# Head-pair keys of batch 0 named ahead of its tail, in a fused linear-attention and feed-forward kernel

## The chip, the cores and the metric

The kernel runs on one core of one Trainium2 chip. The metric is device time in microseconds (us), the median over runs; lower is better. The core has TensorE (PE in the rows; PEld is its weight load), VectorE (DVE), ScalarE (ACT), GpSimd (POOL) and SyncE (SP). SPq and ACTq in the rows are the DMA queues of SyncE and ScalarE.

## The reference

Eight batches of eight heads attend over 576 tokens with 128 random features, and a gated feed-forward layer follows:

```
def phi(x):
    proj = np.einsum('bhsd,df->bhsf', x, w_phi)
    proj = proj - np.max(np.abs(proj), axis=-1, keepdims=True)
    return np.concatenate([np.exp(proj), np.exp(-proj)], axis=-1)
q_p, k_p = (phi(q), phi(k))
kv = np.einsum('bhsf,bhsd->bhfd', k_p, v)
z = np.sum(k_p, axis=2)
num = np.einsum('bhsf,bhfd->bhsd', q_p, kv)
den = np.einsum('bhsf,bhf->bhs', q_p, z)[..., None] + 1e-06
attn = num / den                     # to x: 4608 tokens x 512
h = x @ w_in                         # 512 x 2048
g = h * (1.0 / (1.0 + np.exp(-1.702 * h)))
out = g @ w_out                      # 2048 x 512
```

The inputs are drawn as float32. The weight blocks reach the core 512 KB at a time as 64-bit words, and the kernel turns them into numbers itself.

## The kernel before

**Tiles.** A head pair (hp) is two of the eight heads, so a batch has four pairs. Of a head's 576 tokens 512 are the main part, as 4 groups of 128; the last 64 are the tail. The tails of all heads of a batch are loaded together (`tail_load`, tile `tl`) and made into features in one go (`attn_tail`). Every pair's keys need the tail: the sums over tokens in `keys` take main and tail products into one PSUM bank.

**Precision.** Most operands are split into a high and a low float16 half (`eh` and `el`, `gh` and `gl`, `w16[:, i, 0]` and `[:, i, 1]`), and three products stand for one. For batch 0 the keys of all pairs and the queries of the first half of the tokens (g = 0) go the exact way instead, in float32: `project_whole` turns kt on TensorE against `ident`, multiplies by `wb`, subtracts the maximum (`shifted`), and ScalarE makes the two exponentials. The float16 way (`turned`) writes high and low halves into a tile `xs` and transposes it by DMA into `xT`; the tail and the queries of the second half (g = 1) go that way. Afterwards `across` turns a result of 66 partitions back, and it does so by way of a tile `xs` too.

**Tail queries.** `queries_tail` divides the 64 tail rows of all eight heads. The two heads of a pair lie in the partitions 0 to 63 and 64 to 127. Each half is multiplied, cast and subtracted by itself into a tile `zt`, whose other half has been set to zero once, and `attn_last` brings both to the layout of x with TensorE and the matrix `ii`.

**Weights.** `load_weights(j)` loads block j of w_in and of w_out into `raw`, decodes them on ScalarE and VectorE (through the PSUM tiles `hb` for j below 8) and writes both halves into w16. `moe_chunk` works on up to 384 tokens: products into `hb`, tanh and gate, products into `ab`. The first 512 tokens of batch 0 are done in two parts of eight weight blocks each, so that they can start before all weights are there.

**PSUM.** There are three banks `at` (unordered; `psa()` takes one), two `hb` and three `ab`. In `attention_first` (batch 0), `bank()` takes an `ab`, which the feed-forward layer doesn't need yet.

**Order.** Nothing is issued where it is written. Every operation is recorded in a group, opened by `R.part(v0, v1)`, and `schedule` orders all of them by a planner's costs: it takes, engine by engine, the operation that can start first and, among those that are ready, the one of lowest priority number. The number lies between v0 and v1, by the operation's position in its group and the length of the chain behind it:

```
f = (1 - cp) * i / len(g) + cp * (1 - tail[o] / top)
o.prio = (not o.prio, v0 + (v1 - v0) * f, n)
```

where cp is -0.175 for v0 up to 0.5. For the first 123 groups the pair comes from the table PLACES, by the number of the group, and not from the call. An operation recorded on `two`, `three` or `evac` may go to any of several engines; `price` weighs them. Most tiles have a fixed number of buffers (NB: kt 2, qt 4, vn 2, xs 2, xT 2, raw 3, nf 2, x 3, e 5), which are handed out in the order in which the program names them, unless the name is in `loose` ("sc", "eh", "el", "e", "n1", "cs", "rc", "mq"). All operations carry line 466, where `emit` calls them, so the rows tell them apart by tiles.

**Before the change.** `attention_first` records the weights of the projection (`load_phi`), then the loads of the tail (on ScalarE's queue) and of pair 0, then `attn_tail`, then the four `keys`, the queries of g = 0 and of g = 1, and `queries_tail`.

Of the kernel before, what the change touches and what calls it, by code (L numbers as in the profile page):

```python
# [99 lines left out]
class _Op:  # L100
# [5 lines left out]


PLACES = (
# [25 lines left out]
)  # L134
_READY = {"tensor": 215.0, "scalar": 150.0, "vector": 130.0, "gpsimd": 95.0, "sync": 100.0}

# [38 lines left out]


class Recorder:
    price = dict(tensor=1.000, scalar=0.004, vector=2.234, gpsimd=1.174, sync=1.000)

    def __init__(self, nc):  # L180
        self.nc, self.ops = nc, []
# [291 lines left out]
def attn_moe_fast(ctx, tc, q, k, v, w_phi, w_in, w_out, out):  # L473
# [64 lines left out]
    def new(nm):  # L538
        return R.tile(pools[nm])
# [6 lines left out]
    def new_ex():  # L546

        scr.append(0)
        i = len(scr) % 2
        return scratch[:, 1024 * i : 1024 * i + 1024]  # L550

    def psa():
        return R.tile(at, whole=True)
# [23 lines left out]
    for ap in pools["vts"].aps:  # L577
        nc.vector.memset(ap, 0.0)
        for a in range(2):
            nc.vector.memset(ap[a * D : a * D + D, :, a, 0, D : D + 1], ONE)  # L580
    for ap in pools["zt"].aps:
        nc.vector.memset(ap, 0.0)

    vmx = static("vmx", [P, B], F32)
    wmx = static("wmx", [P, 2 * NJ], F32)
# [221 lines left out]

    def across(src, dst, pat):

        x = new("xs").rearrange("p s i d -> p (s i d)").bitcast(F32)[0:DV]  # L810
        R.evac.copy(x, src)
        tp = psa()[:, 0 : 4 * DV]
        for j in range(4):
            R.tensor.transpose(
                tp[:, j * DV : (j + 1) * DV], x[:, j * P : (j + 1) * P], ident[0:DV, 0:DV]
            )
        R.evac.copy(dst, tp.rearrange(pat, j=2, d=DV))

    def keys(b, hp, kt, vn, tail, nt, exact, keep, bank):
        ekt, eqt, vt, cst = tail  # L820


        if exact:
            tk = project_whole(kt, bank)
            R.three.scale(vn[:, :, 0:D], vn[:, :, 0:D], VS)
            kvt = psa()[0:DV]
            mm = []
            for h in range(2):
                e = new_ex()
                e4 = e.rearrange("p (a s f) -> p a s f", a=4, s=2)  # L830
                R.scalar.activation(e4[:, :, 0], tk[h], AF.Exp)
                R.scalar.activation(e4[:, :, 1], tk[h], AF.Exp, scale=-1.0, bias=-EK * LN2)
                ek = e.rearrange("p (a f) -> p a f", a=4)
                o = kvt[:, 256 * h : 256 * h + 256]
                mm += [(vn[:, 4 * h + t], ek[:, t], o) for t in range(4)]
                for s in range(2):
                    for i, n in ((0, 0), (0, 1), (1, 0)):
                        mm.append((vt[:, hp, h, n], ekt[s][i][:, hp], o[:, s * NF : s * NF + NF]))
            products(mm)
            kf = new("kf")  # L840
            across(kvt, kf, "p (h j d) -> p h j d")
            kf = kf.rearrange("p h s d -> p (h s d)")
# [160 lines left out]
    def queries_tail(nt, cst, x16):  # L1003
# [5 lines left out]
        )  # L1009
        R.vector.reciprocal(rc, rc)  # L1010
        ratio(rc, nt[:, :, D + 1], art[:, 1])
        rcv = rc.rearrange("p (c a) -> p a c", a=2)
        nt4 = nt.rearrange("p (c a) d -> p a c d", a=2)
        xt_ = new("xf").rearrange("p j a d -> p (j a d)")[:, 0 : NHP * D].rearrange(
            "p (c d) -> p c d", c=NHP
        )
        zt = new("zt")
        for a in range(2):
            r = slice(a * D, a * D + D)
            R.two.tensor_mul(  # L1020
                xt_[r], nt4[r, a, :, 0:D], rcv[r, a].unsqueeze(2).broadcast_to([D, NHP, D])
            )
            R.three.copy(zt[r, 0, :, a], xt_[r])
            R.two.tensor_sub(zt[r, 1, :, a], xt_[r], zt[r, 0, :, a])
        attn_last(zt, x16)

    def ratio(rc, z, acc):
# [178 lines left out]
    def attention_first():  # L1206
# [5 lines left out]
        R.part(-20.0, -20.0)  # L1212
        load_phi()
        R.part(-19.9, -19.9)
        tl = tail_load(0, R.scalar)
        nat = [attn_load(0, 0, dv=R.scalar)]
        R.part(-19.8, -19.0)
        nt = new("nt")
        tail = attn_tail(0, tl, bank)
        kk = []  # L1220
        for hp in range(NHP):
            R.part(-19.5 + 0.5 * hp, -19.0 + 0.5 * hp)
            if hp:
                nat.append(attn_load(0, hp))
            kt, qt, vn = nat[hp]
            kk.append(keys(0, hp, kt, vn, tail, nt, EXK[hp], EXQ[0][hp] or EXQ[1][hp], bank))
        for g in range(2):
            for hp in range(NHP):
                w = -17.5 + 0.5 * hp + 8 * g
# [223 lines left out]
```

## Time and profile before

| | us |
|---|---|
| median of three runs | 1065.18 (1064.44 to 1067.8) |
| the profiled execution, its own time | 1066.25 |
| its span, from the first to the last instruction | 1064.5 |
| TensorE busy in the span | 1014.2 |

A row of the timeline gives the start, the duration, the engine, the operation, its output tile and its inputs, how many instructions were merged into it (x8), and in brackets how long the engine had been idle before it and which event ended that. A row of the windows gives a stretch, its length, the busy time of PE, PEld, DVE, ACT and POOL with their instruction counts, the granted TensorE clock as a share of full speed, the DMA share and GB/s. A float32 product is recorded as two instructions.

### The profile page before, as it was taken

To read this page: it belongs to the slowest core of one execution; us is meant where nothing else is said; L and a number is where in the kernel's file an instruction comes from. 1 tells how busy PE (TensorE), PEld (TensorE's weight loads), DVE (VectorE), ACT (ScalarE), POOL (GpSimd) and SP (SyncE) were. 2 spreads that over 40 slices of the span, in tenths; PEclk is the share of its full clock that TensorE was granted. 3 is DMA by queue.
4 is the path that set the end of the run, shared out by engine and by line. 5 is a ranking of instruction groups with operands and counts; after the bars stand their busy time and mean duration, and the time that the engine had idled before them with its cause. 6 is when DMAs were issued, how large, how long until landed. Compare 5 with 4: busy or idle time off the path is not lost.

```text
span 1064.5 us, 24790 instructions
## 1 busy us (share of the span) xinstructions
PE 1014.2 (95%) x9914; PEld 666.7 (63%) x9914; DVE 695.9 (65%) x1278; ACT 663.5 (62%) x1471; POOL 489.2 (46%) x575
## 2 busy tenths in 40 slices
PE   3987999999999999999999999999999999999996
PEld 3655767677665666676666655677766665576543
DVE  5997889887997788888236735656576665223232
ACT  5987989875588698886237735565485554222321
POOL 2218876864387588876006823653463433000000
PEclk6998999999999999999999999999999999999999
DMA  9656264442244264443022321232131120000101
GB/s 262 195 169 176 70 158 110 100 106 61 49 97 94 57 135 94 102 116 76 1 50 62 90 55 31 54 87 51 41 80 23 29 51 11 21 11 1 31 1 33
DMA packets 181021, 80.94 MB, mean 76 GB/s; under 512 B 149536, under 2 KB 174240, under 8 KB 180896
## 3 DMA queue, kind: packets, MB, share of 16 engines
q1 hardware_dynamic: 178048, 78.35, 30.9%
q8 instruction: 79, 1.29, 0.5%
q10 hardware_dynamic: 2848, 0.92, 0.4%
q14 instruction: 46, 0.38, 0.1%
HBM read 45.15 MB, written 9.44 MB: 51 GB/s over the span
## 4 chain that ended last, share of the span: by engine, by line
PE 83%; ACT 6%; DVE 5%; DMA 3%; issue 2%; POOL 1%; ACTq 0%; SPq 0%; DVEq 0%; POOLq 0%
PE ab L466 33%; PE hb L466 32%; PE at L466 17%; DMA xT<-xs 2%; ACT e L466 2%; ACT eh L466 1%; DVE gl L466 1%; DVE sm L466 1%; POOL el L466 1%; ACT x L466 1%; DVE g L466 1%; ACT xs L466 0%; DVE t L466 0%; DMA tl<-in_v_dram 0%; ACT th L466 0%
## 5 line engine op out<-in xcount | busy, mean ns | idle before, releaser
L466 PE MATMUL hb<-x,w 128*128 128x192 f16 (+3 forms) x3264 | 451.7, 279 | 0.7 <-DVE x L466 0.4
L466 PE MATMUL ab<-w,gh 128*128 128x512 f16 x1152 | 337.7, 380 | 0.4 <-ACT gh L466 0.3
L466 PEld LDWEIGHTS <-w 128*128 128x128 f16 x3264 | 276.0, 98 | 95.8 <-issue 1.2
L466 POOL TENSOR_TENSOR el<-e,eh 128x512 f16<-128x512 f32 x168 | 209.1, 1254 | 127.7 <-ACT eh L466 107.0
L466 DVE SCALAR_TENSOR_TENSOR g<-th,hb 128x384 f32<-128x384 f32 (+1 forms) x208 | 107.9, 519 | 179.4 <-ACT th L466 178.6
L466 ACT ACTIVATE th<-hb 128x384 f32<-128x384 f32 (+1 forms) x208 | 96.9, 466 | 193.1 <-PE hb L466 185.1
L466 PE MATMUL ab<-w,gl 128*128 128x512 f16 x576 | 204.3, 379 | 4.2 <-DVE gl L466 4.0
L466 DVE SCALAR_TENSOR_TENSOR gl<-g,gh 128x384 f16<-128x384 f32 (+1 forms) x208 | 136.2, 657 | 50.0 <-ACT gh L466 49.1
L466 PEld LDWEIGHTS <-gh 128*128 128x128 f16 x1152 | 102.4, 98 | 93.9 <-ACT gh L466 16.3
L466 ACT ACTIVATE gh<-g 128x384 f16<-128x384 f32 (+1 forms) x208 | 104.0, 500 | 64.9 <-DVE g L466 64.1
L466 ACT CAST eh<-e 128x512 f16<-128x512 f32 x215 | 128.7, 621 | 3.6 <-PE at L466 3.2
L466 PEld LDWEIGHTS <-eh 128*128 128x128 f16 x1856 | 111.9, 97 | 25.3 <-ACT eh L466 2.7
L466 POOL TENSOR_TENSOR n<-n,cs 128x132 f32<-128x132 f32 (+1 forms) x101 | 58.1, 578 | 98.5 <-ACT n L466 81.1
L466 PEld LDWEIGHTS <-gl 128*128 128x128 f16 x576 | 54.7, 97 | 74.3 <-DVE gl L466 33.2
L466 PEld LDWEIGHTS <-el 128*128 128x128 f16 x928 | 86.2, 98 | 18.7 <-POOL el L466 9.4
L466 PEld LDWEIGHTS <-xT 128*128 128x128 f16 x1056 | 74.6, 99 | 35.9 <-DMA xT<-xs 22.3
L466 PE MATMUL at<-ph,xT 128*128 128x128 f16 x1008 | 94.1, 219 | 0.8 <-DMA xT<-xs 0.6
L466 ACT ACTIVATE e<-t 128x512 f32<-128x512 f32 x128 | 75.9, 625 | 20.2 <-DVE t L466 18.0
L466 ACT ACTIVATE e<-at 128x512 f32<-128x512 f32 x136 | 76.4, 601 | 13.6 <-PE at L466 13.5
L466 PE MATMUL at<-kz,eh 128*128 128x66 f16 x960 | 80.9, 193 | 1.3 <-ACT eh L466 0.7
L466 DVE TENSOR_TENSOR el<-e,eh 128x512 f16<-128x512 f32 x64 | 65.8, 1030 | 24.9 <-ACT eh L466 16.7
L466 PE MATMUL at<-vs,eh 128*128 128x66 f16 x896 | 71.0, 194 | 0.5 <-DVE nf L466 0.5
(179 smaller groups left out, 1349.7 us busy)
## 6 DMA issues: line engine op xcount, KB each, us to landing
raw<-in_moe_w_in_dram SPq DMA_DIRECT2D x16, 512.0 KB, 4.5
raw<-in_moe_w_out_dram SPq DMA_DIRECT2D x16, 512.0 KB, 5.0
kt<-in_k_dram SPq DMA_DIRECT2D x32, 256.0 KB, 2.8
qt<-in_q_dram SPq DMA_DIRECT2D x32, 256.0 KB, 3.1
vn<-in_v_dram SPq DMA_DIRECT2D x62, 128.0 KB, 2.9
out_dram<-e SPq DMA_DIRECT2D x38, 128.0 KB, 2.4
out_dram<-e SPq DMA_DIRECT2D x16, 256.0 KB, 2.6
xT<-xs SPq DMA_TRANSPOSE x68, 2.8
```

The lines of the kernel that those rows point to most:

```text
L466: f(*[g(a) for a in o.args], **{k: g(a) for k, a in o.kw.items()})
```

## The change

Five things change.

1. `keys` is split. The new `keys_front` projects the keys, makes the exponentials and opens the accumulation over the main tokens (eight products, left open); `keys` adds the tail products and closes it. For pairs 0 and 1 of batch 0 the front is named ahead of `attn_tail`, in parts of its own; the load of pair 0 is named ahead of the load of the tail, each in its own part. That makes 126 groups.
2. `attn_tail` of batch 0 takes `at` banks (`psa`) in place of `ab` banks.
3. `across` copies its source into a tile `e` in place of a tile `xs`.
4. `queries_tail` multiplies the reciprocals by a constant `half`, which is 1 for the head that lives in a partition and 0 for the other, and then does one multiplication, one cast and one subtraction over all 512 columns, in place of two of each over 256. The zeros that zt was set to once are now computed, and zt's memset is gone.
5. All places up to the feed-forward layer of batches 2 and 3 are new, and so are three prices.

```diff
-    price = dict(tensor=1.000, scalar=0.004, vector=2.234, gpsimd=1.174, sync=1.000)
+    price = dict(tensor=1.000, scalar=0.001, vector=2.059, gpsimd=1.247, sync=1.000)
...
-    for ap in pools["zt"].aps:
-        nc.vector.memset(ap, 0.0)
+    half = cp.tile([P, 2 * NHP], F32, name="half")
+    nc.vector.memset(half, 0.0)
+    for a in range(2):
+        nc.vector.memset(half[a * D : a * D + D].rearrange("p (c a) -> p c a", a=2)[:, :, a], 1.0)
...
-        x = new("xs").rearrange("p s i d -> p (s i d)").bitcast(F32)[0:DV]
+        x = new("e")[0:DV]
...
+    def keys_front(kt, vn, bank):
+        tk = project_whole(kt, bank)
+        R.three.scale(vn[:, :, 0:D], vn[:, :, 0:D], VS)
+        eks = []
+        for h in range(2):
+            e = new_ex()
+            e4 = e.rearrange("p (a s f) -> p a s f", a=4, s=2)
+            R.scalar.activation(e4[:, :, 0], tk[h], AF.Exp)
+            R.scalar.activation(e4[:, :, 1], tk[h], AF.Exp, scale=-1.0, bias=-EK * LN2)
+            eks.append(e.rearrange("p (a f) -> p a f", a=4))
+        kvt = psa()[0:DV]
+        for h in range(2):
+            o = kvt[:, 256 * h : 256 * h + 256]
+            for t in range(4):
+                R.tensor.matmul(
+                    o, vn[:, 4 * h + t], eks[h][:, t], start=h + t == 0, stop=False,
+                    skip_group_check=True,
+                )
+        return kvt
...
         if exact:
-            tk = project_whole(kt, bank)
-            R.three.scale(vn[:, :, 0:D], vn[:, :, 0:D], VS)
-            kvt = psa()[0:DV]
+            kvt = keys_front(kt, vn, bank) if front is None else front
...
-            products(mm)
+            for i, (st, mv, oi) in enumerate(mm):
+                R.tensor.matmul(
+                    oi, st, mv, start=False, stop=i == len(mm) - 1, skip_group_check=True
+                )
...
+        R.two.tensor_mul(rc, rc, half)
+        xt_ = new("e").rearrange("p (x d) -> p x d", x=2 * NHP)
+        R.two.tensor_mul(
+            xt_, nt[:, :, 0:D], rc.unsqueeze(2).broadcast_to([P, 2 * NHP, D])
+        )
...
+        R.three.copy(zt[:, 0], xt_)
+        R.two.tensor_sub(zt[:, 1], xt_, zt[:, 0])
...
-        tl = tail_load(0, R.scalar)
-        nat = [attn_load(0, 0, dv=R.scalar)]
-        R.part(-19.8, -19.0)
+        nat = [attn_load(0, 0, dv=R.scalar)]
+        R.part(-19.85, -19.85)
+        tl = tail_load(0, R.scalar)
+        NF0 = 2
+        fronts = []
+        for hp in range(NF0):
+            R.part(-19.8 + 0.2 * hp, -19.7 + 0.2 * hp)
+            if hp:
+                nat.append(attn_load(0, hp))
+            fronts.append(keys_front(nat[hp][0], nat[hp][2], bank))
+        R.part(-19.6, -19.0)
         nt = new("nt")
-        tail = attn_tail(0, tl, bank)
+        tail = attn_tail(0, tl, psa)
```

The new places, by group, of those that the prediction speaks of (before, after):

| group | before | after |
|---|---|---|
| load_phi | -91.6 to -64.5 | -319.7 to -277.4 |
| tail load and load of pair 0 | -106.2 to -65.3 (one group) | tail -190.5 to -96.8; pair 0 -292.9 to 143.7 |
| front of pair 0; of pair 1 with its loads | | -328.0 to -90.5; -258.5 to 45.7 |
| attn_tail of batch 0 | -97.6 to -84.4 | -282.9 to -94.9 |
| keys of pairs 0, 1, 2, 3 | -95.6, -94.1, -123.0, -97.6 | -32.8, -29.9, -143.4, -46.2 (starts) |
| queries g = 1 of pairs 0, 1, 2, 3 | -91.0, -97.6, -96.7, -91.7 | -187.2, -111.8, -178.4, -222.1 (starts) |
| weight block 0 | -90.9 to -86.8 | -112.0 to -91.6 |
| weight block 5; 7 | -76.5; -102.2 to -68.2 | -14.5 to 162.4; -2.4 to 438.6 |
| batch 1, pairs 0 to 3 | -28.3, -15.3, -15.8, -87.8 | -278.3, -12.8, -22.0, -157.3 (starts) |
| batch 2, pairs 0 to 3 | -13.5, -86.6, -117.9, -120.6 | -376.6, -122.5, -206.4, -34.9 (starts) |

## Rows read from the trace of the kernel before

**Rows 1.** The page, busy time of each engine

```profile
PE 1014.2 (95%) x9914; PEld 666.7 (63%) x9914; DVE 695.9 (65%) x1278; ACT 663.5 (62%) x1471; POOL 489.2 (46%) x575
```

**Rows 2.** Windows by stage: busy us of each engine, granted clock, DMA share, GB/s

```profile
5.00:21.00 16.00, 0.20 (x4) 0.03 (x1) 7.93 (x17) 9.98 (x18) 1.45 (x2) 0.60 1.07 274
10.00:50.00 40.00, 27.17 (x174) 20.89 (x175) 33.29 (x57) 34.45 (x70) 9.16 (x11) 0.81 0.85 239
30.00:50.00 20.00, 20.00 (x137) 15.31 (x136) 18.09 (x31) 18.35 (x39) 3.11 (x5) 1.00 0.73 216
50.00:60.00 10.00, 9.27 (x61) 6.26 (x60) 9.85 (x18) 9.46 (x22) 1.02 (x2) 1.00 0.42 130
60.00:100.00 40.00, 29.27 (x222) 19.61 (x222) 33.56 (x68) 32.59 (x79) 20.10 (x28) 0.87 0.66 188
79.50:86.00 6.50, 1.68 (x16) 1.41 (x17) 5.02 (x11) 4.88 (x11) 4.43 (x5) 0.78 0.59 162
86.00:97.00 11.00, 9.37 (x108) 6.54 (x107) 8.17 (x17) 9.64 (x29) 9.07 (x11) 0.82 0.88 241
100.00:500.00 400.00, 389.33 (x4612) 269.19 (x4609) 340.14 (x604) 320.82 (x737) 287.12 (x319) 1.00 0.43 97
500.00:1000.00 500.00, 499.88 (x4515) 319.49 (x4514) 258.80 (x485) 250.23 (x540) 169.08 (x180) 1.00 0.18 42
1000.00:1065.00 65.00, 55.25 (x297) 27.35 (x295) 17.94 (x35) 14.77 (x29) 0.00 (x0) 0.96 0.05 14
```

**Rows 3.** Timeline from 20 to 31 us: start, us, engine, instruction, idle before

```profile
21.19 1.14 PE L466 MATMUL ab<-ph,xT 128*128 128x128 f16 x9 [15.98 <-DMA xT<-xs]
...
26.37 1.07 ACT L466 ACTIVATE e<-at 128x512 f32<-128x512 f32 x2
```

**Rows 4.** Timeline of the first 20 us; SPq and ACTq are queues

```profile
6.17 2.55 ACTq L466 DMA_DIRECT2D vn<-in_v_dram  x2
6.42 2.74 SPq L466 DMA_DIRECT2D kt<-in_k_dram  x2
...
8.81 1.28 ACT L466 ACT_TABLE_LOAD   x1 [8.81 <-DMA tl<-in_v_dram]
...
15.50 1.52 SPq L466 DMA_TRANSPOSE xT<-xs  x1
```

**Rows 5.** Timeline around the second hole, from 78.9 us

```profile
78.96 1.05 ACT L466 COPY xs<-at 66x512 f32<-66x512 f32 x2
...
79.58 0.94 PE L466 MATMUL at<-ident,xs 66*128 66x66 f32 x8 [0.54 <-ACT xs L466]
...
80.06 0.40 POOL L466 CAST xs<-qt 128x256 f16<-128x256 f32 x1 [3.32 <-PE at L466]
...
82.61 2.54 SPq L466 DMA_TRANSPOSE xT<-xs  x2
...
85.24 1.03 PE L466 MATMUL ab<-ph,xT 128*128 128x128 f16 x8 [4.71 <-DMA xT<-xs]
```

**Rows 6.** Groups of instructions of the first 100 us

```profile
L466 PE MATMUL at<-x,vn 128*66 128x256 f32 x64 | 16.4, 382 | 1.5 <-ACT x L466 1.1 <-issue 0.3
L466 PE MATMUL ab<-wb,e 128*128 128x256 f32 x48 | 14.6, 424 | 0.0
...
L466 ACT ACTIVATE x<-t 128x512 f32<-128x512 f32 x16 | 9.5, 631 | 0.5 <-DVE t L466 0.4
...
L466 DVE TENSOR_REDUCE sm<-ab 128x4 f32<-128x512 f32 x13 | 8.9, 686 | 1.7 <-PE ab L466 1.6
...
L466 PE MATMUL ab<-ident,kt 128*128 128x128 f32 x16 | 2.9, 313 | 0.5 <-DVE mq L466 0.5
```

**Rows 7.** The tile xf: durations of its instructions, ns, shortest/median/longest

```profile
L466 ACT CAST zt<-xf x15: 388/402/409, 121.5 to 894.2; 64x256 f16<-64x256 f32 x15
L466 POOL TENSOR_TENSOR zt<-xf,zt x13: 663/771/999, 121.9 to 894.8; 64x256 f16<-64x256 f32 x13
L466 POOL TENSOR_TENSOR xf<-nt,rc x12: 608/612/790, 120.1 to 892.9; 64x256 f32<-64x256 f32 x12
```

More of the change, by code (lines that the diff above doesn't have):

```diff
@@ L817, in across, with keys @@
         R.evac.copy(dst, tp.rearrange(pat, j=2, d=DV))
-    def keys(b, hp, kt, vn, tail, nt, exact, keep, bank):
+    def keys_front(kt, vn, bank):
[17 more added lines that the diff above has]
+        return kvt
+    def keys(b, hp, kt, vn, tail, nt, exact, keep, bank, front=None):
         ekt, eqt, vt, cst = tail
         if exact:
-            tk = project_whole(kt, bank)
-            R.three.scale(vn[:, :, 0:D], vn[:, :, 0:D], VS)
-            kvt = psa()[0:DV]
+            kvt = keys_front(kt, vn, bank) if front is None else front
             mm = []
             for h in range(2):
[L829 to L833, printed above, removed]
                 o = kvt[:, 256 * h : 256 * h + 256]
-                mm += [(vn[:, 4 * h + t], ek[:, t], o) for t in range(4)]
                 for s in range(2):
@@ L1011, in queries_tail @@
         ratio(rc, nt[:, :, D + 1], art[:, 1])
[L1012 to L1015, printed above, removed]
-        )
[L1017 to L1024, printed above, removed]
+        R.two.tensor_mul(rc, rc, half)
+        xt_ = new("e").rearrange("p (x d) -> p x d", x=2 * NHP)
+        R.two.tensor_mul(
+            xt_, nt[:, :, 0:D], rc.unsqueeze(2).broadcast_to([P, 2 * NHP, D])
+        )
+        zt = new("zt").rearrange("p t c a d -> p t (c a) d")
+        R.three.copy(zt[:, 0], xt_)
+        R.two.tensor_sub(zt[:, 1], xt_, zt[:, 0])
+        zt = zt.rearrange("p t (c a) d -> p t c a d", a=2)
         attn_last(zt, x16)
@@ L1222, in attention_first @@
             R.part(-19.5 + 0.5 * hp, -19.0 + 0.5 * hp)
-            if hp:
+            if hp >= NF0:
                 nat.append(attn_load(0, hp))
             kt, qt, vn = nat[hp]
-            kk.append(keys(0, hp, kt, vn, tail, nt, EXK[hp], EXQ[0][hp] or EXQ[1][hp], bank))
+            kk.append(
+                keys(0, hp, kt, vn, tail, nt, EXK[hp], EXQ[0][hp] or EXQ[1][hp], bank,
+                     fronts[hp] if hp < NF0 else None)
+            )
         for g in range(2):
```

51 rows, old and new, of the table PLACES are left out of this document.

## The prediction

> **What bounds the kernel now.** I read the page's busy times first. TensorE is busy 1014.2 us [rows 1] of a span of 1064.5; every other engine stays under 700. So the question is where TensorE is not busy, and the windows by stage answer it [rows 2]. From 500 to 1000 us it idles 0.12 us, from 100 to 500 us 10.7 us in all. Before that: 15.8 us between 5 and 21 us, 0.7 us between 50 and 60, 10.7 us between 60 and 100. The last stretch, from 1000 on, idles 9.75 us after the final products; nothing in the diff is there. A gain must therefore come out of the first 100 us, and a loss can only be new idle time of TensorE somewhere before 500.
>
> The second thing to see in [rows 2] is that ScalarE and VectorE are nearly as full as TensorE while it is fed: 9.46 and 9.85 us of the ten from 50 to 60. Between 10 and 50 us ScalarE works 34.45 of 40 and VectorE 33.29; TensorE has no idle time at all from 30 to 50. So three engines share the bound of the opening stage, and work given to one early is worth only what the others can follow.
>
> Then I looked for the two holes. The first ends at 21.19 us: TensorE has waited 15.98 us for the transposed tail xT of batch 0 [rows 3]. The keys of head pair 0, which need no DMA transpose, come behind it in TensorE's order. In the queues [rows 4], SP issues kt at 6.42 us, after weight blocks, and the DMA transpose of the tail at 15.50; ScalarE issues vn until 8.72 us, and loads its table until 10.09. The second hole is at 79.5 to 86 us, where TensorE works 1.68 of 6.5 us [rows 2]. The rows around it [rows 5] tell a chain: the last two results of the exact queries are copied into xs at 78.96 us, TensorE turns them from there at 79.58, only then does GpSimd write the next query into xs at 80.06 (it waited 3.32 us for TensorE), the transposes are issued at 82.61, and TensorE goes on at 85.24 after 4.71 us of idling. xs has two buffers, handed out in program order, so results and queries queue for the same two.
>
> **Two fronts ahead of the tail.** A front is one head pair's keys without the tail products: four transposes, four products with wb, eight with vn. By the groups of the first 100 us [rows 6] (four head pairs there; wb also serves the queries, so 8 of its 48 records are one front's): 2.9/4 + 14.6 x 8/48 + 16.4/4 = 7.3 us of TensorE, 14.5 us for two. Its ScalarE work is four exponentials at 0.63 us (16 in that group), and at most a copy and a scale of about that size: 2.5 to 3.7 us. Its VectorE work is two maxima at 0.69 and two subtractions of the same size: 2.8 us. The products themselves do not get more or fewer; they move.
>
> What the move is worth is bounded three ways. By TensorE alone: 14.5 us of work into a hole of 15.8 us, so at most 14.5. From below: nothing, if kt comes no earlier. By ScalarE: it does not begin before 8.8 us [rows 4], because its own DMA issues stand in front of it, so it cannot use the hole's first half. From 10 to 50 us it could pack its 34.45 us at the density of its fullest row, 0.946 [rows 2]: 34.45/0.946 = 36.4 us instead of 40, a gain of 3.6 us. This bound is nearer than TensorE's, since TensorE has no spare in 30 to 50 only because it is late, and I take it. VectorE by the same density would give 40 - 33.29/0.946 = 4.8 us, so it does not bind first.
>
> The start of ScalarE moves as well. The six tail loads have priorities from -190 to -97 on its queue; the two vn loads, third and fourth of a part that runs from -292.9 to 143.7, come out at about -75 and +53 by the recorder's formula, so the second one falls behind arithmetic that is ready. Two issues take 2.55 us [rows 4], one 1.3: I take 1.3 us for the earlier table load. Behind that late vn load wait the second head's products of front 0; their data is not needed until its exponentials are done, so this costs nothing unless the load slips past some 15 us.
>
> On SP, kt of pair 0 (-292.9) and of pair 1 (about -258) now pass the weight blocks, whose first has -112. The weight data comes later by those bytes, but ScalarE and VectorE have the fronts to do meanwhile.
>
> The Trainium skill speaks against this term: its page "DMA: Bandwidth & Descriptors", section "Issuing engines are not separate DMA queues", says that transfers issued from any engine run on the same 16 DMA engines and interleave. By that rule a reordering of loads gains nothing while those engines are full, and both terms above would fall away. The trace half agrees: 274 GB/s and a DMA share of 1.07 from 5 to 21 us, 0.85 from 10 to 50 [rows 2]. Only half, because ScalarE stood still behind its own DMA issues until 8.72 us [rows 4], whatever had landed; I keep it as a rival.
>
> **The open accumulators.** Two fronts hold two of the three `at` banks until the tail's features exist, and the tail now projects through `at` too. Its three steps then pass through one bank in turn. Before, with the `ab` banks, they already took from 21.19 to 27.44 us [rows 3], one behind the other; so I add nothing. If the tail is no earlier than before, TensorE has the other two pairs' projections for that time, and these use `ab`. The bound above: those 6.3 us idle.
>
> **Own tile for turned results.** `across` now writes into e, which has five buffers in no fixed order. The query may enter xs before the last result has been turned, and the transpose lies behind TensorE's other work. TensorE could get back 4.8 us (6.5 - 1.68), and nothing if another buffer of fixed order holds the query (nf is one). ScalarE limits it here too: from 79.5 to 97 us it works 4.88 + 9.64 us, which at 0.946 fills 15.35 of 17.5 us. I take 2.15 us.
>
> **Tail results in one masked operation.** Per batch [rows 7]: before, two multiplications (0.61), two casts (0.40) and two subtractions (0.77), 3.6 us. After, one of each over 512 columns, which I bound by the two of 256 (3.6 again), and a product of 8 columns with `half`, bounded by one of 256 (0.61): from 0 to 0.6 us more a batch. Both lie on ScalarE and GpSimd beside a TensorE that idles 10.7 us in 400; 0 us, and 0.6 us at most, batch 0's own. The memset of zt goes and those of `half` come, at a time when VectorE waits for data: 0.
>
> **New order.** It cannot be read from the diff which engine waits where; a list of new places has no sign that I can derive. From above: the 10.7 us of 60 to 100 and the 10.7 of 100 to 500 could vanish or double. I take 0 and keep it in the range.
>
> **Sum.** The profiled execution took 1066.25 us (span 1064.5 and 1.75 around it). 1066.25 - 3.6 - 1.3 - 2.15 = 1059.2. The median of the runs, 1065.18, lies 1.07 below that execution; so the median after should be 1058.1, 0.67% faster. About 0.3% (3.2 us) is what a measurement of this kernel tells from no change.
>
> **Rivals.** *The start is bound by transfers.* This is the rule above as a mechanism: kt comes early, the weights come as much later, ScalarE starves for them where it starved for the tail. For it: the DMA share of 1.07. Against it: 0.73 from 30 to 50 us, and ScalarE's late start is due to its own queue. Only the 2.15 us are left: 1063.0, no change that can be told. That the fronts are issued early but wait for ScalarE's DMA issues ends in the same place.
>
> *TensorE was the bound after all.* It has no idle time from 30 to 50 us [rows 2]; if the fronts are done at 21 us, that stretch is shorter by their 14.5 us less what ScalarE can't follow. Half of that bound and the 4.8 us of the second hole: 7.3 + 4.8 = 12.1, which gives 1053. Against it: ScalarE's 18.35 of those 20 us.
>
> *Weights late (slower).* Block 5 stood at -76.5, behind one head pair of batch 1 and three of batch 2; now it stands at -14.5 to 162, behind three of batch 1 and four of batch 2, and block 7 (-2.4 to 439) behind all eight. raw has three buffers in program order, so every later block waits as well. The first chunk of the feed-forward needs blocks 0 to 7. Until it runs, TensorE idles 0.27 of the time (60 to 100 us [rows 2]). ScalarE's 34.45 + 9.46 + 32.59 us from 10 to 100, over batch 0's four pairs, is at most 19 us a pair, conversions included; three pairs more ahead of block 5 delay it by up to 57 us. It decides from 7.05/0.27 = 26 us of delay. At 45 us: 12.2 us lost, 7.05 gained, 1070. Against it: x has three buffers too, so batches 1 and 2 cannot run far ahead.
>
> **Chances.** Forecast 0.40, TensorE's bound 0.20, transfers 0.22, weights late 0.18. The first two are faster by over 0.3%, 0.60; transfers the same, 0.22; the last slower, 0.18. The range goes from 1050 (below the 1053 by the unknown order) to 1069, which leaves out most of the last case and little else. For the faster cases alone it is 1050 to 1062.
>
> **What would show it.** Right: TensorE's first product with kt before 12 us, two groups of x,vn products before the tail's xT; ScalarE's table load about 1 us earlier; no 4 us gap at the first query of the second half; 100 to 500 us idle about 10 us as before. Wrong: TensorE at half clock and idle until 20 us with ScalarE waiting for raw; the first dense hb products later than 97 us; new gaps behind gl or w between 100 and 500.

## The result and the profile after

The changed kernel takes 1051.78 us at the median (1050.94 to 1052.36) against 1065.02: a ratio of 0.987, interval 0.9851 to 0.9889, so it is 13.2 us faster. Measured again later, the ratio was 0.9851 (0.9827 to 0.9875). The forecast was 1058.1. The time lies in the range, on the side that was forecast, but the gain is almost twice the 7 us of the sum and nearest to the rival that named TensorE as the bound (1053).

The page's busy times of the changed kernel, to be read against [rows 1]:

```profile
PE 1013.7 (97%) x9914; PEld 667.6 (64%) x9914; DVE 733.7 (70%) x1465; ACT 651.6 (62%) x1449; POOL 283.2 (27%) x396
```

And its windows, with the columns of [rows 2] (stretch, its length, busy time of TensorE, weight load, VectorE, ScalarE and GpSimd, granted clock, DMA share, GB/s):

```profile
5.00:21.00 16.00, 12.75 (x49) 8.71 (x48) 9.46 (x17) 9.62 (x20) 1.88 (x3) 0.79 1.11 294
10.00:50.00 40.00, 35.32 (x209) 25.13 (x208) 33.19 (x57) 34.18 (x71) 7.29 (x9) 0.91 0.87 224
...
50.00:60.00 10.00, 7.79 (x67) 5.98 (x65) 9.93 (x22) 8.45 (x23) 0.66 (x2) 1.00 0.64 206
60.00:100.00 40.00, 31.05 (x287) 21.55 (x288) 37.35 (x84) 37.91 (x89) 17.68 (x28) 0.91 0.63 166
79.50:86.00 6.50, 5.92 (x89) 4.81 (x89) 6.38 (x17) 6.19 (x19) 4.02 (x6) 1.00 0.45 116
...
100.00:500.00 400.00, 392.28 (x4913) 277.80 (x4912) 375.76 (x756) 340.45 (x782) 194.86 (x242) 1.00 0.48 106
500.00:1000.00 500.00, 499.17 (x4176) 311.13 (x4176) 260.70 (x507) 216.32 (x461) 60.03 (x80) 1.00 0.15 35
```

TensorE is as busy as before, 1013.7 against 1014.2 us, in a span of 1049.5 against 1064.5: nearly all of the gain is idle time, 50.3 to 35.8 us. By stage it went as in the table. Its last column is a second profile of the changed kernel, taken with the later measurement. There TensorE's 9914 instructions were busy 2.1 us less, the idle time to 60 us is 2.3 us more, and the later stages differ by 0.5 us or less. So the figures of the first 60 us are good to some 2 us only. The first profiles of the two kernels also lie 15.3 us apart, 2 more than the medians.

| stage | TensorE idle before | after | forecast of the difference | after, second profile |
|---|---|---|---|---|
| 5 to 21 us | 15.8 | 3.25 | | 6.7 |
| to 60 us in all | 19.5 | 10.6 | -4.9 | 12.9 |
| 60 to 100 us | 10.7 | 8.95 | -2.15 | 9.4 |
| 100 to 500 us | 10.7 | 7.7 | 0 | 8.2 |
| 500 us to the end | 9.4 | 8.5 | 0 | 8.8 |

The first hole shows it in the timeline (SPq and ACTq are queues), where [rows 3] and [rows 4] stood:

```profile
2.01 1.10 SPq L467 DMA_DIRECT2D kt<-in_k_dram  x2
...
4.39 1.28 ACT L467 ACT_TABLE_LOAD   x1 [4.39 <-issue]
...
5.79 1.08 PE L467 MATMUL ab<-ident,kt 128*128 128x128 f32 x4 [0.20 <-DMA kt<-in_k_dram]
...
6.66 1.82 ACTq L467 DMA_DIRECT2D vn<-in_v_dram  x2
...
8.52 0.59 ACT L467 COPY e<-ab 128x512 f32<-128x512 f32 x1 [2.53 <-DMA qt<-in_q_dram]
...
9.25 2.74 PE L467 MATMUL ab<-wb,e 128*128 128x256 f32 x8 [2.38 <-ACT e L467]
9.52 0.41 ACT L467 CAST xs<-qt 128x256 f16<-128x256 f32 x1
...
12.71 3.88 SPq L467 DMA_TRANSPOSE xT<-xs  x2
...
17.25 3.67 PE L467 MATMUL at<-x,vn 128*66 128x256 f32 x16
...
24.50 0.61 PE L467 MATMUL at<-ph,xT 128*128 128x128 f16 x8
```

SP issues kt at 2.01 us, ScalarE loads its table at 4.39, and TensorE turns the keys of pair 0 at 5.79, where it had idled until 21.19. ScalarE's copy then waits until 8.52, because its own vn loads stand in front of it (6.66 + 1.82 us); the runs with these loads on SP, below, bear this out. Two projections and the first front's eight products with vn (sixteen records) lie ahead of 21 us; the tail's xT is used at 24.50. A second thing is new: a query of the second half is written into xs at 9.52 us already and transposed with the tail at 12.71.

The forecast's bound was ScalarE's density, and there it fails. From 10 to 50 us ScalarE is no denser than before, 34.18 against 34.45 us, and yet TensorE has idled 8.9 us less by 60 (6.6 in the second profile). What ScalarE did in these 60 us is different. Its three decoding steps of the weights, groups of the first 60 us of the kernel before:

```profile
L466 ACT ACTIVATE hb<-raw 128x512 f32<-128x512 f32 x14 | 8.9, 637 | 2.0 <-DMA raw<-in_moe_w_out_dram 1.3 <-DMA raw<-in_moe_w_in_dram 0.4 <-DVE w L466 0.2
L466 ACT ACTIVATE raw<-raw 128x512 int32<-128x512 uint16 x12 | 7.9, 668 | 0.0
L466 ACT CAST w<-hb 128x512 f16<-128x512 f32 x12 | 6.9, 585 | 2.2 <-DVE hb L466 2.2
```

and of the changed kernel:

```profile
L467 ACT ACTIVATE hb<-raw 128x512 f32<-128x512 f32 x10 | 6.3, 634 | 0.4 <-DVE w L467 0.4
L467 ACT ACTIVATE raw<-raw 128x512 int32<-128x512 uint16 x9 | 6.0, 671 | 0.0
L467 ACT CAST w<-hb 128x512 f16<-128x512 f32 x9 | 5.3, 590 | 2.1 <-DVE hb L467 2.1
```

38 steps became 28, 23.7 us became 17.6: decoding was put off and ScalarE fed TensorE in that time. From 60 to 100 us ScalarE was busy 37.91 of 40 us against 32.59, a density of 0.948, the same as the 0.946 that the forecast took from the fullest row. But by 100 us it had not caught up. The first eight blocks, decoded through hb, were done in both kernels, while the blocks behind them (wy) were further back than before. Windows of the first 100 us, the kernel before and then the changed one:

```profile
0.00:100.00 100.00, 69.78 (x496) 50.66 (x497) 79.03 (x154) 77.69 (x168) 32.98 (x78) 0.86 0.73 205
```

```profile
0.00:100.00 100.00, 80.44 (x607) 58.26 (x608) 83.11 (x176) 83.61 (x186) 28.32 (x75) 0.93 0.74 199
```

and two of ScalarE's decoding groups in these 100 us, again before and after:

```profile
L466 ACT ACTIVATE raw<-raw 128x512 int32<-128x512 uint16 x21 | 13.9, 671 | 0.0
...
L466 ACT ACTIVATE wy<-raw 128x512 f32<-128x512 f32 x8 | 5.4, 671 | 0.8 <-POOL w L466 0.7
```

```profile
L467 ACT ACTIVATE raw<-raw 128x512 int32<-128x512 uint16 x17 | 11.6, 685 | 0.0
...
L467 ACT ACTIVATE wy<-raw 128x512 f32<-128x512 f32 x3 | 2.1, 710 | 0.0
```

With the casts into w, ScalarE's decoding to 100 us was 65 steps and 41.3 us before, 54 steps and 34.6 us after. Without it ScalarE had done 36.4 us of other work by then, and 49.0 after the change. Of these 12.6 us more, 6.7 are decoding put off past 100 us, and 5.9 are a ScalarE that was busier in all.

### The profile page after: what moved, and what is told of

Same layout as the page of the kernel before. It is cut to its first block, busy times and chain, and to the rows that moved or that the text cites. A ratio compares the mean times of both kernels' runs of the same rounds, so it can differ in the third digit from the quotient of the medians.

```text
span 1049.5 us, 24669 instructions
## 1 busy us (share of the span) xinstructions
PE 1013.7 (97%) x9914; PEld 667.6 (64%) x9914; DVE 733.7 (70%) x1465; ACT 651.6 (62%) x1449; POOL 283.2 (27%) x396
## 4 chain that ended last, share of the span: by engine, by line
PE 83%; DVE 6%; ACT 6%; issue 2%; DMA 1%; POOL 0%; SPq 0%; ACTq 0%; DVEq 0%; POOLq 0%
PE ab L467 34%; PE hb L467 32%; PE at L467 17%; ACT e L467 1%; DVE el L467 1%; DVE wy L467 1%; DVE hb L467 1%; ACT x L467 1%; DVE gl L467 1%; ACT eh L467 1%; ACT w L467 1%; DMA tl<-in_v_dram 0%; DMA qt<-in_q_dram 0%; DVE sm L467 0%; DVE t L467 0%
## 5 line engine op out<-in xcount | busy, mean ns | idle before, releaser
L467 PE MATMUL ab<-w,gl 128*128 128x512 f16 x576 | 207.8, 379 | 1.5 <-DVE gl L467 1.4
L467 DVE SCALAR_TENSOR_TENSOR gl<-g,gh 128x384 f16<-128x384 f32 (+1 forms) x208 | 120.1, 578 | 46.0 <-ACT gh L467 45.2
L467 DVE TENSOR_TENSOR el<-e,eh 128x512 f16<-128x512 f32 x161 | 116.1, 738 | 15.2 <-ACT eh L467 11.0
L467 POOL TENSOR_TENSOR el<-e,eh 128x512 f16<-128x512 f32 x71 | 86.7, 1224 | 109.3 <-ACT eh L467 76.5
L467 PE MATMUL at<-ph,xT 128*128 128x128 f16 x1024 | 94.9, 220 | 2.0 <-DVE t L467 1.0
L467 PEld LDWEIGHTS <-el 128*128 128x128 f16 x928 | 85.7, 98 | 15.3 <-DVE el L467 4.5
L467 POOL TENSOR_TENSOR n<-n,cs 128x132 f32<-128x132 f32 (+1 forms) x74 | 42.4, 576 | 159.0 <-ACT n L467 144.5
L467 PE MATMUL at<-kz,eh 128*128 128x66 f16 x960 | 78.7, 193 | 1.9 <-DVE x L467 0.7
```

Source lines behind the costliest of these rows:

```text
L467: f(*[g(a) for a in o.args], **{k: g(a) for k, a in o.kw.items()})
```

## Experiments

Most of these kernels keep the planner's order, its buffers and its choice of engines and change one thing behind it, because a new plan moves everything at once. `held(order, late, behind)` is a stable sort of the finished order: the operations `late` come behind all of `behind`, what depends on them or reuses their buffers follows, all else stays. A loss is given as the ratio's distance to 0.987, in us of 1065; against the second measurement of the changed kernel (0.9851) each is 2 us more.

**The fronts behind the tail.** A small product that reads xT stands ahead of the first front, so that TensorE waits for xT there; its result is overwritten.

```diff
         self.order = self.schedule()
+        tail = [o for o in self.order if o.tag == "tail" and o.eng == "sync"]
+        late = [o for o in self.order if o.tag == "front" and o.eng == "tensor"]
+        self.order = self.held(self.order, late, tail)
...
+            if o is gate:
+                self.nc.tensor.matmul(tp[:, 0:D], xT[:, 0], xT[:, 0, 0:D], start=True, stop=True)
```

> The changed kernel with its own order, buffers and engine choices, but the two fronts' TensorE work waits for the tail's transposed xT, as all key work of batch 0 did before; what depends on it moves back with it and all else stays. If the fronts in TensorE's first hole are the main gain, about 9 us are lost (1061). If ScalarE's packing sets their worth, as the prediction had it, 4 to 5 us (1056 to 1057). If the new order gains elsewhere and the place of the fronts matters little, under 3 us (below 1055).

0.9955 (0.9943 to 0.9966): 9 us lost. Windows of this run:

```profile
5.00:21.00 16.00, 2.31 (x13) 1.67 (x11) 1.26 (x4) 2.78 (x6) 1.89 (x4) 0.61 0.92 244
...
100.00:500.00 400.00, 391.40 (x4827) 274.65 (x4825) 375.25 (x755) 340.67 (x780) 193.79 (x242) 1.00 0.49 109
```

TensorE works 2.31 us of the 16, but ScalarE only 2.78 and VectorE 1.26: their queues stand behind the front too. So the run takes more away than the hole of TensorE, and a second one puts decoding ahead of the fronts.

```diff
+        tail += [o for o in self.order if o.tag == "decode"][:18]
```

> As in the run with the fronts held behind the tail's xT, but they also stand behind the decoding of the first three weight blocks, so that ScalarE and VectorE have that work to do while TensorE waits, as they had before the change. If the 9 us lost there were TensorE's, 7 to 9 us are lost again (1059 to 1061). If ScalarE and VectorE standing behind the held fronts made them, only 3 to 5 us (1055 to 1057).

0.9939 (0.9917 to 0.9961): 7.3 us lost, now with ScalarE at 9.11 and VectorE at 8.02 of the 16 us, close to the 9.98 and 7.93 of [rows 2]:

```profile
5.00:21.00 16.00, 1.19 (x5) 0.79 (x5) 8.02 (x14) 9.11 (x18) 1.87 (x3) 0.58 1.05 266
...
100.00:500.00 400.00, 392.37 (x4836) 276.73 (x4834) 376.54 (x755) 340.48 (x780) 194.97 (x241) 0.99 0.48 108
```

So 7.3 us are lost when TensorE's hole is back with the other engines at work, more than the 4.9 forecast. In this run TensorE works 40.60 us in the first 60, as in the kernel before (40.51), and 31.01 from 60 to 100, as in the changed kernel (31.05): the loss lies where the fronts stood. In both runs 100 to 500 us stay as in the changed kernel (391.4 and 392.4 us busy, 389.3 before): what was gained there does not come from the fronts.

**The order of the loads.**

```diff
+        raw = [o for o in self.order if o.tag == "raw"][:3]
+        late = [o for o in self.order if o.tag == "kq" and o.eng == "sync"]
+        self.order = self.held(self.order, late, raw)
```

> The changed kernel, but SP issues the first three weight blocks ahead of kt and qt of pairs 0 and 1, as before the change. If the order of the loads makes the gain of the start, kt lands some 6 us later and most of 6 us is lost (1056 to 1058). If the start is bound by transfers in sum, what is lost on the keys is gained on the weights: within 2 us of 1051.8.

0.9897 (0.9867 to 0.9926): 2.9 us, between the two expectations, and the interval overlaps that of the changed kernel. The trace is clearer: from 5 to 21 us TensorE works 6.52 us, against 12.75 and 9.34 in the two profiles of the changed kernel. So the order of the loads is part of what fills the first hole, though how much of that reaches the total is not clear of the noise.

**The query and the turned results.** First in the changed kernel, then the own tile alone in the kernel before.

```diff
+        turn = [o for o in self.order if o.tag == "turn"]
+        late = [o for o in self.order if o.tag == "query"]
+        self.order = self.held(self.order, late, turn)
```

> The changed kernel, but the queries of the second half of batch 0 may enter xs only behind the last turned result in the program's order, as two shared buffers had enforced. If the own tile is what closed the second hole, 2 us (ScalarE's bound) to 4.8 us (TensorE's) are lost: 1054 to 1056.6. If other work now covers the transpose, nothing: 1051.8.

0.9924 (0.99 to 0.9947): 5.8 us lost, more than either number. The second hole is there again, as in [rows 5], in this run's timeline:

```profile
76.03 1.04 PE L510 MATMUL ab<-ph,xT 128*128 128x128 f16 x8 [3.77 <-DMA xT<-xs]
```

and in its window from 60 to 100 us:

```profile
60.00:100.00 40.00, 26.82 (x228) 18.27 (x228) 30.61 (x71) 30.55 (x76) 14.73 (x27) 0.79 0.58 158
```

```diff
-        x = new("xs").rearrange("p s i d -> p (s i d)").bitcast(F32)[0:DV]
+        x = new("xs")                       # planned as before
+        x.tl.own = owns[len(turns) % 4]     # but written elsewhere
```

> The kernel before, its order unchanged; only the turned results go into buffers of their own (space of the x tile of batch 1, which is not in use yet) and no longer into xs. GpSimd then needn't wait 3.3 us for TensorE ahead of the first query of the second half. The prediction has this part at 2.15 us (1063); TensorE's whole second hole would be 4.8 us (1060.2); without a new order nothing, if SP or ScalarE hold the transpose back anyway (1065).

1.0012 (1.0 to 1.0023): nothing gained. The timeline of this run around the second hole tells why:

```profile
76.15 0.86 POOL L467 CAST xs<-qt 128x256 f16<-128x256 f32 x1
...
80.56 0.39 ACT L467 CAST xs<-qt 128x256 f16<-128x256 f32 x1
...
84.90 1.03 PE L467 MATMUL ab<-ph,xT 128*128 128x128 f16 x8 [4.80 <-DMA xT<-xs]
```

GpSimd writes its query at 76.15 us in place of 80.06 [rows 5], but the next cast stands in ScalarE's fixed order at 80.56, and TensorE waits 4.80 us for the transpose, as before. The tile is worth something only together with an order that uses it; the changed order writes the first query 70 us earlier.

**Both taken back.** The edits of the second and of the query run together.

> The changed kernel with both moves taken back at once: the fronts stand behind the tail's xT and three decoded weight blocks, and the queries of the second half enter xs behind the last turned result. Taken back singly they lost 0.7 and 0.5 per cent of the time. If they are two independent parts that make nearly all of the gain, 12 to 14 us are lost together, and 0 to 3 us of the gain are left for the places after 100 us: ratio 0.997 to 1.000. If they overlap, because a front that is late leaves room for the query's transpose, 8 to 10 us: ratio 0.995.

1.0008 (0.9994 to 1.0022): all of the gain is gone, as if the two were independent, and nothing is left for the rest. Its windows say that this is not quite so:

```profile
60.00:100.00 40.00, 23.26 (x170) 16.29 (x170) 29.64 (x64) 30.11 (x71) 8.05 (x15) 0.79 0.59 174
100.00:500.00 400.00, 392.33 (x4786) 275.75 (x4784) 377.17 (x759) 340.94 (x784) 197.33 (x246) 0.99 0.48 110
```

From 100 to 500 us TensorE is as full as in the changed kernel, 392.3 us, 3 more than before. From 60 to 100 us it works 23.26, 6 less than before. The new order with both taken out is worse there than the old one, so a loss of this kind can overstate what a part brought. It shows with the query alone as well, where TensorE works 26.82 us from 60 to 100 against 29.27 before; with the fronts alone it does not (31.01).

**What bounds the opening stage.** Single steps are done twice, in both kernels: ScalarE's hb<-raw for the first eight loads into raw (blocks 0 to 3 of w_in and w_out), or the key projections of batch 0 on TensorE.

```diff
-            f(*[g(a) for a in o.args], **{k: g(a) for k, a in o.kw.items()})
+            for _ in range(2 if o.tag == "twice" else 1):
+                f(*[g(a) for a in o.args], **{k: g(a) for k, a in o.kw.items()})
```

> The kernel before, with one decoding step of ScalarE (hb<-raw) done twice for the first eight weight blocks: 8 times 0.64, 5.1 us more ScalarE work ahead of about 45 us, nothing else moved. If ScalarE's load bounds the opening stage, as the prediction had it, 4 to 5 us are lost. If TensorE's order bounds it there and decoding can wait, under 2 us.

1.0033 (1.0019 to 1.0047): 3.5 of 5.1 us.

> The kernel before, with the four transposes and the four wb products of each head pair's key projection of batch 0 done twice: by the rows about 2.1 us at full clock for a pair, 8.6 us of TensorE, between 22 and 57 us. If TensorE's work behind its first hole bounds that stage, 6 to 9 us are lost; if ScalarE does, under 3 us.

1.0051 (1.0033 to 1.0069): 5.4 of 8.6 us. Neither engine is the bound alone: some two thirds of what is added on either shows in the time.

> The changed kernel with the same 5.1 us of ScalarE work added. If the fronts moved the bound of the opening stage from TensorE to ScalarE, 4 to 5 us are lost here and more than in the kernel before. If ScalarE bounds neither, under 2 us.

0.9896 (0.9879 to 0.9914): 2.8 us of 5.1 by the first measurement of the changed kernel, 4.8 by the second. The first number falls between the two expectations, the second within the one that has ScalarE as the new bound; the changed kernel was not measured beside this run, so which holds is open.

> The changed kernel with the key projections of batch 0 done twice, as in the kernel before: 8.6 us more of TensorE's work, half of it in its first hole. If TensorE's hole now has room for it, under 3 us are lost against the changed kernel (5.4 us in the kernel before). If the chain of each front, TensorE then ScalarE then TensorE, sets the pace, 4 to 6 us.

0.9927 (0.9902 to 0.9951) against 0.9851 for the changed kernel, run beside it on the same chip: 8 us, against the expectation that the hole has room. TensorE's timeline of this run:

```profile
9.46 3.69 PE L469 MATMUL ab<-wb,e 128*128 128x256 f32 x16 [2.58 <-ACT e L469]
...
18.44 3.67 PE L469 MATMUL at<-x,vn 128*66 128x256 f32 x16
```

and of the changed kernel beside it:

```profile
9.88 3.75 PE L467 MATMUL ab<-wb,e 128*128 128x256 f32 x8 [3.60 <-ACT e L467]
...
18.76 3.45 PE L467 MATMUL at<-x,vn 128*66 128x256 f32 x15 [1.73 <-ACT vn L467]
```

Up to 18.4 us the doubled work costs nothing beside that execution: sixteen wb records take 3.69 us here, eight took 3.75 there, at half the granted clock, and the products with vn start at 18.44 and 18.76 (17.25 in the first profile). So the hole did have room, and the loss is made later. Pairs 2 and 3 add about 4.3 us of work there, by estimate half of the 8.6, which is half of the loss; the other half stays open. This profile can't settle it, since it is of the fastest execution of the run, 5.3 us above the changed kernel's.

**ScalarE's loads.** The two vn loads of pair 0 are issued by SP, then the tail's v loads as well.

```diff
         self.order = self.schedule()
+        for o in self.order:
+            if o.tag == "vn" and o.eng == "scalar":
+                o.eng = "sync"
```

> The changed kernel, but the two loads of vn of pair 0 are issued by SP and not by ScalarE, whose queue they hold until 8.48 us. If ScalarE's own DMA issues set the beginning of its arithmetic, its copy starts near 6.9 us in place of 8.52 and 1 to 2 us are gained (1050 to 1051). If the transfers are limited in sum, nothing moves (1051.8).

0.9848 (0.9831 to 0.9864). The copy that stood at 8.52 us:

```profile
6.35 0.58 ACT L471 COPY e<-ab 128x512 f32<-128x512 f32 x1 [0.40 <-PE ab L471]
```

> The changed kernel itself, unchanged, beside the other runs of this call, so that they can be compared on one chip: ratio 0.987 to the kernel before, as first measured.

0.9851 (0.9827 to 0.9875).

> The changed kernel with the two loads of vn of pair 0 on SP's queue, a second time and beside the changed kernel: ScalarE's first copy moved from 8.52 to 6.35 us there. If ScalarE's own issues hold the beginning back, it is again 2 us faster than the changed kernel in the same call; if the first 2 us were the chip's, no difference.

0.984 (0.9816 to 0.9864).

> The tail's v loads on SP's queue as well, so that ScalarE issues four loads and not eight. If every issue on ScalarE costs, another 0.6 to 1.2 us against the run with vn alone. If SP's queue is now what is late (its vn loads reach until 10.5 us and delay the second weight block), nothing or a loss of 1 us.

0.9838 (0.9814 to 0.9862). Medians: 1052.32 for the changed kernel, 1051.16 and 1051.13 for these two. The copy did move, by 2.2 us between the first profiles and by 2.0 side by side (9.15 to 7.12). About 1 us of that arrives in the total where the kernels ran side by side, and the tail's loads on SP bring nothing more; the first run stood 2.3 us below the first measurement of the changed kernel, but not beside it. The intervals overlap, so a gain in time is not shown; if there is one, it is 0.1 to 0.2%. TensorE's granted clock from 5 to 21 us was higher too, 0.89, 0.89 and 1.00 in the three runs against 0.79, and may hold a part of it.

**The tail results in halves.**

```diff
+            if o.tag == "half":
+                for a in range(2):
+                    r = slice(a * D, a * D + D)
+                    f(*[g(x)[r].rearrange("p (c a) d -> p c a d", a=2)[:, :, a] for x in o.args])
```

> The changed kernel with the multiplication, the cast and the subtraction of the tail results done as two of 256 columns each in the same places of the order, and zt's memset back. The prediction has this part at 0: within 1 us of 1051.8. If the single masked operation had shortened a chain that TensorE waits for, up to 0.6 us for each of eight batches: 1056.6.

> The tail results in halves once more, in five rounds. If the single masked operation is worth nothing, as the prediction had it, ratio 0.985 to 0.987 as for the changed kernel. If it is worth the 1 to 4 us that the first three rounds hinted at, 0.988 to 0.990.

0.9881 (0.9855 to 0.991), then 0.9887 (0.9867 to 0.9907): 1.2 and 1.8 us lost, or 3 to 4 against the second measurement. All four differences point the same way, though no pair of intervals is clear of the other. TensorE's first product with zt, and ScalarE's casts to zt ahead of it, in the timeline of the second of these runs:

```profile
70.21 0.83 ACT L471 CAST zt<-e 64x256 f16<-64x256 f32 x2
...
72.23 0.39 PE L473 MATMUL at<-ii,zt 128*128 128x64 f16 x8 [2.57 <-ACT e L473]
```

and in that of the changed kernel beside it:

```profile
70.27 0.62 ACT L467 CAST zt<-e 128x512 f16<-128x512 f32 x1
...
71.97 0.61 PE L467 MATMUL at<-ii,zt 128*128 128x64 f16 x8 [2.23 <-ACT e L467]
```

It waits 2.57 us here and 2.23 there: 0.34 us in batch 0, on TensorE's path. In both the wait ends not with zt but with a copy from `at` into e (at 71.62 here, 71.35 there): by the trace the product waits for a bank of `at`. That copy stands in ScalarE's queue behind the casts to zt, two in 0.83 us here and one in 0.62 there. Where the rest of the loss is made stays open.

**The division of the subtractions el.** In the changed kernel VectorE has 161 of them and GpSimd 71; before it was 64 and 168.

```diff
+        for i in range(97):
+            el[i * len(el) // 97].eng = "gpsimd"     # in the kernel before: "vector"
```

> The changed kernel with 97 of VectorE's 161 subtractions el given back to GpSimd, evenly over the kernel and in the same places of the order, which is the division of before. If the shift from GpSimd to VectorE made the 3 us of idle time that TensorE lost between 100 and 500 us, about 3 us come back (1055). If the order made it, under 1 us.

1.0135 (1.0118 to 1.0152): 28 us lost.

> The kernel before with 97 of GpSimd's 168 subtractions el moved to VectorE in the same places of the order, which is the division of after. If that division is worth 3 us by itself, 1062; if it only fits the new order, 1065 or more, since VectorE was at 85% from 100 to 500 us already.

1.0118 (1.0101 to 1.0135): 12.6 us lost. The window from 100 to 500 us, of the changed kernel with GpSimd's share put back:

```profile
100.00:500.00 400.00, 382.93 (x4612) 261.80 (x4611) 354.45 (x663) 327.17 (x742) 259.56 (x289) 0.99 0.45 103
```

and of the kernel before with VectorE's share:

```profile
100.00:500.00 400.00, 383.79 (x4502) 262.61 (x4500) 352.31 (x653) 315.02 (x722) 210.69 (x253) 1.00 0.42 95
```

Both lose 5 to 9 us of TensorE there. The division belongs to its order, and evenly chosen moves break it in either direction; so the runs do not tell whether the division or the order made the 3 us. No run has the old prices with the new places.

## Why the prediction was wrong

- *The two holes.* Right, both: where TensorE idled, what ended it, and that the diff fills them.
- *Two fronts, bounded by ScalarE from 10 to 50 us (3.6 us).* This is the step that failed: the bound counted all of ScalarE's 34.45 us as work that must be done in that stretch, to be packed closer or not at all. ScalarE was not packed closer there (34.18 of 40 us, where it was 34.45). TensorE gained all the same, 8.9 us to 60 us with the start of ScalarE, against 4.9 forecast for the two terms; the second profile has 6.6, the held fronts 7.3 to 9. What the sum lacked is that decoding is not due yet: to 60 us ScalarE did 6.1 us less of it, and 6.7 us were still put off at 100. That the room for the fronts came from there is read from the two traces; no run leaves the fronts early and puts the decoding back. The density of 0.946 was reached from 60 to 100 us only; from 10 to 100 us it was 80.54/90 = 0.895. The forecast's rule over these 90 us, 76.5/0.946 = 80.9, would have given 9.1 us, near the measured gain, but by luck, since neither the density nor the work was the same.
- *VectorE as the bound.* The prediction set it aside by its rows from 10 to 50 us. From 10 to 100 us it worked 33.29 + 9.85 + 33.56 = 76.7 us before, as much as ScalarE's 76.5, and the change loads it more. No run adds work to VectorE alone, so this rival is open.
- *The earlier start of ScalarE.* Its table came 4.4 us earlier. Its first long step came 1.6 us earlier (the copy at 8.52 us, against the first decoding step at 10.11), and the 1.3 was near that, but not for the reason given: not one vn load fell behind arithmetic that was ready, but both, and one of the tail, fell behind the table load, and both vn loads still stand ahead of the copy. That its own loads hold it back is shown by the copy at 6.35 us with vn on SP.
- *Own tile, 2.15 us.* The stage from 60 to 100 us gave 1.8 (1.4 in the second profile). The size was near by luck, as the mechanism was named too narrowly: not a transpose that is a little earlier, but a query that is prepared 70 us earlier, which the places decide. Alone in the old order the tile is worth nothing.
- *Masked operation, 0.* Too low, probably: 1 to 4 us, not settled.
- *New order, 0.* 3 us from 100 to 500 us (2.5 in the second profile), kept in every run that spoiled only the opening; of what kind is open.
- *Open accumulators.* Nearly as forecast: in the tail TensorE waits 0.27 us, at 27.49 us, until VectorE has read a result out of `at`. By the same reading a bank of `at` holds TensorE up later, when the accumulators are long closed: 2.23 us until 71.33 us, when a turned result has been copied into e.
- *Rivals.* Bound by transfers: no. The DMA share from 5 to 21 us was 1.07 before and 1.11 after, the engines full in both, and yet TensorE works 12.75 us there in place of 0.20, and half of that (6.52) with the old order of the loads. So what lands first counts for the start even then; in the total it is 2.9 us, not clear of the noise. The rule of the Trainium skill that stood behind this rival ("DMA: Bandwidth & Descriptors", "Issuing engines are not separate DMA queues") is about which engine issues a transfer; that a reordering gains nothing was the prediction's own step from it. That section of the Trainium skill says as well that issuing on several engines saves only the issuing time, which is usually small relative to the DMA itself. The trace agrees: the two vn loads hold ScalarE for 1.82 us and land 5.6 us after their issue (median). But that time stands in the queue of an engine that TensorE waits for; without it a copy comes 2.2 us earlier, of which the total shows 1 to 2 at most. TensorE as the bound: nearest in time, but in the kernel before ScalarE's added work costs as large a part of itself as TensorE's. Weights late: they were later, and up to 500 us TensorE waited 0.3 us for them.

## What to carry to other kernels

When an engine's density is used as a bound, ask of each kind of its work when the bound engine needs it: work that can be put off comes off the sum, and the bound holds for the rest. A buffer of its own is worth what the order makes of it, so try the pair and not the buffer alone. Undoing a part of a planned order can overstate that part. And a stage read from one execution is as good as a second execution of the same kernel says, here to some 2 us in the opening.

## What the runs showed of the hardware

TensorE's granted clock in the opening differs from one execution to the next. The first eight wb records of the same program took 2.74 us in one profile and 3.75 in the other. Windows around them, of the first of these executions:

```profile
5.00:9.00 4.00, 1.67 (x10) 1.03 (x8) 0.28 (x1) 1.46 (x3) 0.00 (x0) 1.00 1.05 329
9.00:13.50 4.50, 3.59 (x12) 2.66 (x12) 3.78 (x7) 1.86 (x6) 0.81 (x1) 0.64 1.23 281
```

of the changed kernel beside the later runs:

```profile
5.00:9.00 4.00, 0.63 (x4) 0.42 (x4) 0.28 (x1) 0.97 (x2) 0.00 (x0) 0.78 1.01 307
9.00:13.50 4.50, 3.62 (x9) 2.83 (x10) 2.23 (x4) 1.72 (x4) 0.81 (x1) 0.50 1.23 293
```

and of the run with doubled projections:

```profile
5.00:9.00 4.00, 1.12 (x9) 0.86 (x8) 0.28 (x1) 1.22 (x3) 0.00 (x0) 1.00 1.06 317
9.00:13.50 4.50, 4.04 (x21) 3.61 (x22) 2.62 (x5) 1.45 (x4) 0.81 (x1) 1.00 1.14 283
```

Half clock is the level of 1.2 GHz, 1.00 that of 2.4. The changed kernel ran its first products at the lower level in one execution and partly in the other; in the one profile with the projections doubled TensorE kept the upper level, so twice the work took the same time. That the doubling kept it there is not shown: with the vn loads of pair 0 and the tail's v loads on SP and nothing doubled, the clock from 5 to 21 us was 1.00 as well. What TensorE had worked in the four us before does not order the three: 0.63 us went ahead of 0.50, 1.12 ahead of 1.00, but 1.67 ahead of 0.64. How far the clock explains the 0.3% between single times of one kernel was not measured.
